# Value loads over all partitions, an accumulated output and halving sums in a fused attention and gated-MLP kernel

## The chip, the cores and the metric

The kernel runs on one core of one Trainium2 chip. The metric is device time in microseconds for one execution; the median of three runs is 217.5 us (216.51 to 218.15). Engine names below: PE is the matrix engine, PEld its weight load, DVE the VectorE, ACT the ScalarE, POOL the GpSimd, SP the SyncE, which here only issues DMAs. A `DMA_TRANSPOSE` is a DMA that transposes 2-byte data on its way.

## What is computed

```python
def _A_ref(x, wqkv, wo):                 # S 2048, D 512, 32 heads of 16
    W, dil = 8, 2                        # key w of row s is row s - 2 w
    q, k, v = split(x @ wqkv)
    logits = einsum("bhsd,bhswd->bhsw", q, kg) * Dh ** -0.5   # masked where s - 2 w < 0
    attn = softmax(logits, axis=-1)
    o = einsum("bhsw,bhswd->bhsd", attn, vg)
    return o @ wo

def _B_ref(x, w1, w2, w3, w4):           # F 1376
    h = gelu(layernorm(x) @ w1)
    hs = concat(h's four column groups, shifted by +1, -1, +2, -2 rows) @ w2
    x1 = x + hs
    return x1 + gelu(layernorm(x1) @ w3) @ w4

x = A_x
xn = layernorm(x)
s = _A_ref(xn, A_wqkv, A_wo)
g = silu(_B_ref(xn, B_w1, B_w2, B_w3, B_w4))
return x + s * g
```

All inputs and the output are bf16; the output is 2048 rows of 512.

## The kernel before

The 2048 rows are cut into 16 tiles of 128 rows (index `i`) and 4 chunks of 512 rows (index `c`, four tiles each). The weights lie in SBUF from the start on. Nothing is scheduled by a planner at build time: the string `ORDER` lists some 810 steps, `name.arguments`, and the loop at line 700 issues them one after the other. Each engine, and each engine's DMA queue, works through its own instructions in that order and stops at the first whose inputs are not ready or whose buffer is not free. So a step that waits holds up all that stands behind it on its engine, SP's queue included, which carries nearly all loads and every transpose.

The steps, in the order in which a tile goes through them:

- `ldx`, `ldxc` load x (tiles 0 to 3 one by one, then whole chunks); `ldqk`, `ldv`, `ldw1` to `ldw4`, `ldwo` load weights. `st` takes the row statistics of x on DVE, `rs` and `r2` turn them into 1/std on POOL, `nm` normalizes on ACT into `xr[i]`, `xT` transposes that by DMA into `xnT`. Chunk 0 goes a shorter way over PE (`nm0`, `tr0`, `ev0`).
- `qk` (8 blocks a chunk) and `v` are PE products; `eqk` and `ev` copy them out of PSUM on ACT. `sv` writes the value tile to `v_dram` in DRAM, by a POOL DMA, in (dim, head) order.
- `pw(c, u)` multiplies q by k shifted by 2u rows on DVE (128x2048 elements); `lg(c, u)` sums over head dims with 16 small PE products into the PSUM tile `lg` (8 offsets x 128 rows, heads and tiles on partitions). `smx` subtracts the maximum (DVE), `ex` exponentiates (ACT), `sms` sums over the offsets and inverts (DVE), `smn` multiplies, reordering into `E_n`, and `tE` transposes `E_n` by two DMAs into `att`.
- `vl(i, u)` loads the value rows of tile `i` shifted by 2u from `v_dram`: partition group u % 4 (32 partitions), in four blocks of 32 rows. Eight loads of 128 KB fill the buffer `vs` of one tile; there are three such buffers. `vp` multiplies `vs` by `att` on DVE, `ws` sums over the offsets with 8 PE products against the 0/1 matrix `sel`, `eo` copies out, `oTr` transposes two tiles by DMA, `wo` is the last product of the attention. The last two tiles go over PE instead (`oTp`, `eoT`).
- `w1`, `eh`, `hTr`, `w2`: the first part of the MLP, with the shifts as column offsets of `hT`; `xa` adds the residual on DVE, `st3s`, `r3`, `nm3`, `x1Tr` are its second normalization and transpose; `w3` (11 blocks a chunk), `eg`, `w4` (11 products a tile), `ya`, `si` give g in `xr[i]`.
- `sg` multiplies s (PSUM) by g on DVE into `xr[i]`; `fag` on POOL or `fav` on DVE adds x; `so` writes the 128 rows of the tile to the output.

PSUM has six banks `mm0` to `mm5` for products and the `lg` tile; the last argument of a PE step is its bank. A bank is free again once DVE or ACT has read it, which is how a late DVE instruction stops PE.

The lines that the change touches are 475 to 522 (softmax), 616 to 644 (value loads, product, sum), 145 to 171 and 187 (the buffers of x), 277 (`sel`), 693 (`fag`) and `ORDER`.

Of the kernel before, what the change touches and what calls it, by code (L numbers as in the profile page):

```python
# [8 lines left out]
AF = mybir.ActivationFunctionType  # L9
ALU = mybir.AluOpType  # L10
# [30 lines left out]
w2.8.3 ev.11 st3s.10 hTr.12 w3.0.9.0 smx.1 sv.11 vl.5.1 v.14.2 eg.0.9 vl.5.2 vl.3.7 w3.0.1.4
vl.4.3 xa.8 w3.0.6.0 vl.4.0 eg.0.1 st3s.6 vl.4.2 w2.12.3 vl.3.0 eg.0.6 st3s.5 r3.3 vl.4.7 ev.14
w3.0.5.4 pw.2.2 vl.5.3 ex.1 vl.3.1 w2.13.2 vl.5.6 xa.12 vl.5.5 w3.0.8.0 st3s.8 vl.3.3 vl.5.4
xa.13 sv.14 w3.0.4.3 nm3.6 vl.3.5 r3.2 st3s.12 vl.5.0 eg.0.8 w3.0.3.2 st3s.13 vl.3.2 vl.4.4
w3.0.0.1 sms.1 vl.5.7 w3.0.2.5 eg.0.3 vl.4.1 eg.0.5 xT.15 w3.0.7.2 r3.6 eg.0.2 vp.3 w3.0.10.4
eg.0.7 eg.0.4 lg.2.1 lg.2.2 eg.0.10 lg.2.0 w2.11.3 eg.0.0 pw.2.3 nm3.5 w4.0.1 nm3.4 xa.11 nm3.7
x1Tr.2 smn.1 st3s.11 pw.2.5 w4.3.3 r3.5 tE.1.0 ya.0 tE.1.1 pw.2.4 si.0 qk.3.7.1 x1Tr.3 ya.3
w4.2.4 eqk.3.7 si.3 vp.5 qk.3.3.1 v.15.3 eqk.3.3 ya.2 w3.1.0.2 vp.4 ev.15 w1.15.4 nm3.10 sv.15
eg.1.0 qk.3.0.3 qk.3.1.1 eh.15 qk.3.6.5 nm3.11 hTr.15 ws.5.4 eqk.3.0 ws.4.2 eo.5 vl.8.5 ws.3.3
vl.7.4 lg.2.5 eo.3 qk.3.4.4 vl.6.6 eo.4 vl.6.0 si.2 qk.3.5.3 vl.7.6 vl.6.1 w2.15.2 vl.7.0 vl.6.4  # L50
eqk.3.5 w2.14.0 xa.15 vl.6.7 eqk.3.6 vl.6.3 w4.1.3 eqk.3.1 st3s.15 vl.8.4 eqk.3.4 xa.14 vl.6.5
vl.7.3 st3s.14 vl.8.6 vl.7.5 w3.1.10.0 r3.7 ya.1 vl.7.7 vl.6.2 w3.1.7.4 eg.1.10 vl.8.0 vl.7.2
w3.1.1.3 vl.8.3 vl.8.2 w3.1.3.1 eg.1.7 vp.6 vl.8.7 w3.1.6.0 vl.8.1 eg.1.3 oTr.1 w3.1.4.4 eg.1.6
w3.1.5.1 eg.1.4 vl.7.1 ws.6.0 x1Tr.5 eg.1.5 lg.2.3 eg.1.1 lg.2.4 pw.2.6 w3.1.8.1 si.1 vl.9.4
wo.0.3 pw.2.7 vl.9.2 vl.9.7 wo.1.4 eo.6 vl.9.0 vp.7 eg.1.8 vl.9.3 wo.3.0 oTr.2 wo.2.5 nm3.15
qk.3.2.1 sg.3 vl.9.6 nm3.14 sg.2 fag.3 vl.9.1 ws.7.0 eqk.3.2 sg.1 vl.9.5 lg.2.6 eo.7 lg.2.7
vl.10.6 w3.1.9.1 pw.3.0 fag.2 vl.10.1 vl.10.3 w3.1.2.0 fag.1 eg.1.9 smx.2 vl.10.2 vl.10.4 w2.9.4
eg.1.2 vl.10.5 so.g.2 vl.10.7 w4.4.0 so.g.1 oTr.3 so.g.3 sg.0 ex.2 xa.9 fag.0 pw.3.2 x1Tr.7
w4.7.4 so.g.0 st3s.9 vl.10.0 ya.4 r3.4 sms.2 si.4 lg.3.0 w4.6.0 pw.3.3 nm3.9 smn.2 w4.5.3 nm3.8
pw.3.1 tE.2.1 ya.6 x1Tr.4 ya.7 lg.3.3 si.6 lg.3.1 wo.4.0 ya.5 si.7 pw.3.6 tE.2.0 si.5 wo.5.3  # L60
sg.4 wo.6.4 sg.5 fag.4 wo.7.0 sg.6 nm3.13 w3.2.2.3 pw.3.4 fag.5 nm3.12 w3.2.9.4 x1Tr.6 eg.2.2
so.g.4 vp.10 w3.2.5.1 fag.6 w3.2.4.5 eg.2.5 so.g.5 so.g.6 w3.2.3.3 sg.7 eg.2.4 vp.8 fag.7
ws.10.0 eg.2.3 lg.3.2 eg.2.9 vl.13.2 w3.2.1.5 so.g.7 eo.10 vl.13.1 vl.13.7 w3.3.0.4 eg.2.1 vp.9
vl.13.6 vl.13.5 w3.2.8.0 eg.3.0 vl.13.0 w3.2.7.5 vl.13.4 eg.2.8 vl.13.3 pw.3.5 w3.2.6.4 eg.2.7
lg.3.6 eg.2.6 lg.3.4 lg.3.5 pw.3.7 w3.2.10.5 w3.2.0.4 eg.2.10 lg.3.7 eg.2.0 ws.9.5 smx.3 ws.8.0
eo.9 vl.12.5 w4.10.4 vl.11.3 eo.8 vl.11.7 oTr.4 ex.3 w4.8.0 ya.10 vl.11.4 vl.11.1 vl.11.0 si.10
vl.11.5 sms.3 vl.11.2 w4.11.4 vl.11.6 vl.12.4 vl.12.2 ya.8 vl.12.7 smn.3 si.8 vl.12.1 wo.8.0
ya.11 tE.3.1 vp.11 w4.9.5 si.11 vl.12.0 vl.12.6 vl.12.3 tE.3.0 sg.8 w3.3.5.4 ya.9 fag.8 w3.3.8.0
si.9 eg.3.5 wo.9.5 so.g.8 w3.3.4.3 sg.9 vp.12 w3.3.2.1 fag.9 eg.3.4 w3.3.10.4 eg.3.2 so.g.9
eg.3.8 w3.3.6.3 eg.3.10 vp.13 ws.12.0 eg.3.6 w3.3.9.4 eo.12 vl.15.1 vl.15.0 w3.3.1.0 vl.15.3  # L70
eg.3.9 vl.15.2 w3.3.7.3 vl.15.4 eg.3.1 vl.15.5 w3.3.3.4 eg.3.7 vl.15.7 vl.15.6 ws.11.0 eg.3.3
ws.13.3 eo.11 vl.14.6 w4.15.4 vl.14.5 eo.13 vl.14.0 vp.15 vl.14.7 oTr.5 w4.14.3 ya.15 oTr.6
# [8 lines left out]
def kernel(  # L81
# [32 lines left out]
    U4 = 4  # L114
    T32 = 32
    NB = P // T32
    NPW, NVS, NH3, NVT, NHT = 3, 3, 12, 3, 3

    x2 = A_x.flatten_outer_dims()
    out2 = out.flatten_outer_dims()  # L120
# [613 lines left out]
```

## Time and profile before

| | |
|---|---|
| median of the runs | 217.5 us (216.51 to 218.15) |
| the profiled execution | 216.87 us, of which the span is 215.1 |
| PE, DVE, ACT, POOL busy | 190.6, 161.6, 132.2, 78.8 us |
| granted PE clock | 0.99 of full speed |
| DMA: SP's queue, share of 16 engines' span | 33.24 MB, 70.8% |
| DMA: POOL's queue | 3.95 MB, 6.0% |
| value loads `vs<-v_dram` | 128 of 128 KB, 3.6 us median from issue to landing (2.1 to 7.5) |
| value stores `v_dram<-vt` | 16 of 128 KB, 3.7 us median |
| output stores from POOL | 14 of 128 KB, 2.7 us median |
| `DMA_TRANSPOSE` `xnT<-xr` | 12, 3.9 us median (2.4 to 8.4) |

The page is of one execution. Matmuls are pipelined, so that their busy times overlap; the pace of PE is read from the distance of starts. A group line gives the source line, the engine, the operation, what is written and read, how often, then busy us and mean ns of one, then the idle time just before and what ended it.

### The profile page before, as it was taken

The numbers are of one execution on the slowest core, as the hardware profiler recorded it, in microseconds if no ns is written. First come the engines' busy times: TensorE is split into PE (matmuls) and PEld (weight loads), VectorE is DVE, ScalarE is ACT, GpSimd is POOL, SyncE is SP. The second block draws the span as 40 slices with busy tenths as digits, with TensorE's granted clock in tenths as the row PEclk, the third lists the DMA queues.
The fourth block names the chain that finished last, engine by engine and source line by source line (L and its number), as shares of the span: only waits on it lengthen the run. The fifth ranks groups of instructions, "written<-read, shape, count | busy, mean of one in ns | idle before, by whom it ended". The sixth has DMA issues, their size and how long they took to land.

```text
span 215.1 us, 3828 instructions
## 1 busy us (share of the span) xinstructions
PE 190.6 (89%) x1408; PEld 85.5 (40%) x1408; DVE 161.6 (75%) x203; ACT 132.2 (61%) x198; POOL 78.8 (37%) x129
## 2 busy tenths in 40 slices
PE   6899769999897989996999979988988996998990
PEld 1444323444342434452444434434444442443440
DVE  4887977199798399969933369999999686826593
ACT  3267865687848825992499588743764950972240
POOL 7146974621163402712310202940691001700282
PEclk9999988999999999999999999999999999999999
DMA  6999998899847698993317999992536499079212
GB/s 197 362 290 378 342 166 197 220 203 247 136 98 123 142 202 193 251 167 73 73 33 213 239 226 214 215 235 47 96 119 184 110 213 167 24 224 221 70 49 98
DMA packets 63011, 37.95 MB, mean 176 GB/s; under 512 B 38371, under 2 KB 61521, under 8 KB 62993
## 3 DMA queue, kind: packets, MB, share of 16 engines
q1 hardware_dynamic: 60976, 33.24, 70.8%
q0 software_dynamic: 1472, 3.95, 6.0%
q10 hardware_dynamic: 544, 0.52, 0.8%
q8 instruction: 11, 0.18, 0.3%
q14 instruction: 8, 0.06, 0.1%
HBM read 24.84 MB, written 4.21 MB: 135 GB/s over the span
## 4 chain that ended last, share of the span: by engine, by line
DVE 29%; PE 28%; DMA 19%; SPq 11%; issue 6%; POOL 3%; ACT 2%; DVEq 0%; ACTq 0%; POOLq 0%
SPq L620 9%; DVE vs L629 8%; DMA vs<-v_dram 7%; DVE pw L456 6%; PE mm L376 6%; PE mm L582 5%; PE mm L400 4%; DMA xnT<-xr 4%; DMA xc<-in_A_x_dram 3%; PE mm L599 3%; PE mm L641 3%; PE mm L679 2%; DVE xr L686 2%; DVE st L299 2%; DVE ssum L497 2%
## 5 line engine op out<-in xcount | busy, mean ns | idle before, releaser
L629 DVE TENSOR_TENSOR vs<-vs,att 128x4096 bf16<-128x4096 bf16 x16 | 39.6, 2487 | 15.1 <-DMA vs<-v_dram 13.7
L456 DVE TENSOR_TENSOR pw<-qT,kT 128x2048 bf16<-128x2048 bf16 x32 | 39.1, 1258 | 12.4 <-ACT kT L385 5.9
L582 PE MATMUL mm<-x1T,w_sb 128*128 128x512 bf16 (+1 forms) x176 | 40.7, 379 | 1.8 <-DVE xr L686 1.7
L599 PE MATMUL mm<-w_sb,h 128*128 128x512 bf16 (+1 forms) x176 | 39.9, 379 | 2.5 <-DVE xr L538 1.7
L591 ACT ACTIVATE h<-mm 128x512 bf16<-128x512 f32 (+1 forms) x44 | 25.2, 597 | 13.5 <-PE mm L582 13.2
L694 POOL TENSOR_TENSOR xr<-xc,xr 128x512 bf16<-128x512 bf16 x9 | 17.6, 1958 | 42.3 <-DVE xr L686 42.2
L376 PE MATMUL mm<-xnT,wqk_sb 128*128 128x512 bf16 x128 | 30.4, 384 | 0.6 <-DVE xr L606 0.6
L599 PEld LDWEIGHTS <-h 128*128 128x128 bf16 (+1 forms) x176 | 16.9, 98 | 23.8 <-issue 3.9
L582 PEld LDWEIGHTS <-w_sb 128*128 128x128 bf16 (+1 forms) x176 | 17.2, 100 | 22.2 <-issue 2.8
L610 ACT ACTIVATE xr<-xr 128x512 bf16<-128x512 bf16 x16 | 10.0, 632 | 23.9 <-DVE xr L606 23.7
L418 POOL DMA_DIRECT2D v_dram<-vt x16 | 9.7, 605 | 36.9 <-ACT vt L410 36.7
L400 PE MATMUL mm<-wv_sb,xnT 128*128 128x512 bf16 x64 | 18.4, 414 | 2.2 <-DMA xnT<-xr 1.5
L376 PEld LDWEIGHTS <-wqk_sb 128*128 128x128 bf16 x128 | 12.4, 99 | 16.2 <-issue 2.0
L531 PE MATMUL mm<-w_sb,hT 128*128 128x512 bf16 x64 | 16.1, 379 | 1.3 <-DMA hT<-ht 1.1
L425 PE MATMUL mm<-w_sb,xnT 128*128 128x512 bf16 x64 | 15.8, 379 | 1.2 <-ACT ht L435 1.2
L329 POOL TENSOR_SCALAR ve<-mv 128x2 f32<-128x2 f32 (+1 forms) x11 | 4.2, 379 | 34.3 <-DVE mv L543 28.0
L538 DVE TENSOR_TENSOR xr<-mm,xr 128x512 bf16<-128x512 f32 x16 | 10.7, 677 | 7.4 <-PE mm L531 7.4
L559 ACT ACTIVATE xn<-xr,nmr,rstd 128x512 bf16<-128x512 bf16 x16 | 12.4, 813 | 5.4 <-POOL nmr L336 4.0
L679 PE MATMUL mm<-wo_sb,oT 128*128 128x512 bf16 x64 | 15.3, 379 | 0.3 <-DVE xr L606 0.3
L467 PE MATMUL lg<-pw,e_log 128*32 128x128 bf16 x512 | 12.5, 223 | 3.3 <-DVE pw L456 3.2
L330 POOL TENSOR_TENSOR rstd<-ve,mhalf 128x2 f32<-128x2 f32 (+1 forms) x15 | 14.7, 980 | 1.2
L410 ACT ACTIVATE vt<-mm 128x512 bf16<-128x512 f32 x16 | 9.5, 594 | 7.2 <-PE mm L400 6.9
(71 smaller groups left out, 247.0 us busy)
## 6 DMA issues: line engine op xcount, KB each, us to landing
vs<-v_dram SPq DMA_DIRECT2D x128, 128.0 KB, 3.6
v_dram<-vt POOLq DMA_DIRECT2D x16, 128.0 KB, 3.7
out_dram<-xr POOLq DMA_DIRECT2D x14, 128.0 KB, 2.7
xc<-in_A_x_dram SPq DMA_DIRECT2D x3, 512.0 KB, 9.0
w_sb<-in_B_w_dram SPq DMA_DIRECT2D x2, 688.0 KB, 10.6
w_sb<-in_B_w_dram SPq DMA_DIRECT2D x2, 640.0 KB, 10.6
wqk_sb<-in_A_wqkv_dram SPq DMA_DIRECT2D x2, 512.0 KB, 6.0
wv_sb<-in_A_wqkv_dram ACTq DMA_DIRECT2D x2, 256.0 KB, 3.7
```

Source lines behind the costliest of these rows:

```text
L376: nc.tensor.matmul(pt, lhsT=wqk_sb[:, dt, nt * P : (nt + 1) * P], rhs=xnT[c][:, :, dt, :], start=(dt == 0), stop=(dt == ND - 1),)
L400: nc.tensor.matmul(pt, lhsT=xnT[c][:, jj, dt, :], rhs=wv_sb[:, dt, :], start=(dt == 0), stop=(dt == ND - 1),)
L425: nc.tensor.matmul(pt, lhsT=xnT[c][:, jj, dt, :], rhs=w1_sb[:, dt, :], start=(dt == 0), stop=(dt == ND - 1),)
L456: nc.vector.tensor_tensor(out=pw_t[c, u], in0=q_t[c], in1=k_t[c][:, :, DIL * u : DIL * u + CH], op=ALU.mult)
L531: nc.tensor.matmul(pt, lhsT=hT[:, g, r0 : r0 + P], rhs=w2_sb[:, g, :], start=(g == 0), stop=(g == ND - 1),)
L582: nc.tensor.matmul(pt[:fs, :], lhsT=w3_sb[:, dt, ft * P : ft * P + fs], rhs=x1T[c][:, :, dt, :], start=(dt == 0), stop=(dt == ND - 1),)
L591: nc.scalar.activation(h3[c, ft][:fs, :], mm.pop(("w3", c, ft))[:fs, :], AF.Gelu_apprx_tanh)
L599: nc.tensor.matmul(pt, lhsT=h3[c, ft][:fs, jj * P : (jj + 1) * P], rhs=w4_sb[:fs, ft, :], start=(ft == 0), stop=(ft == NF - 1),)
L620: nc.sync.dma_start(out=vs[i][T32 * (u % U4) : T32 * (u % U4) + T32, :, u // U4, :], in_=v_dram[r0 : r0 + P, :].rearrange("(b t) d -> t b ...
L629: nc.vector.tensor_tensor(out=vv, in0=vv, in1=att[c][:, :, H * jj : H * jj + H].unsqueeze(2).to_broadcast([P, NB * 2, DH, H]), op=ALU.mult,)
L679: nc.tensor.matmul(pt, lhsT=oT[i // 2][:, i % 2, dt, :], rhs=wo_sb[:, dt, :], start=(dt == 0), stop=(dt == ND - 1),)
L694: nc.gpsimd.tensor_tensor(out=xr[i], in0=xtile(i), in1=xr[i], op=ALU.add)
```

## The change

- `vl` becomes `vl(i, h, b)`: one load covers offsets 4h to 4h+3 of the 32 rows of block b, on all 128 partitions (partition 4t + u for row t, offset u). The source is an access pattern whose rows overlap. There are again eight loads of 128 KB a tile. `E_n`, `sel`, `vp` and `ws` follow that layout.
- Thirteen tiles of the output are first filled with x by four DRAM-to-DRAM copies (`pre`); `soa` then adds `s * g` to them by an accumulating DMA from POOL, in place of `fag` and `so`. Tiles 13, 14 and 15 still go by `fav` and `so`.
- `sms` adds halves (512, 256, 128 elements a partition) in place of one strided reduction; `smn` becomes two instructions.
- Chunks 1 and 3 of x share a buffer; there are 14 buffers for `h3` in place of 12.
- `ORDER` is made anew. Some of what moves: `ldw3` and `ldw1` change places among the first loads, `ldqk.s.0` comes after `ldqk.s.1`, `ldw3.s.0`, x's chunk 1 and `ldw4.s.2`; `st.4` and `st.5` come ahead of `st.8`; `ldxc.s.3` and `ldw4.s.1` come later; the softmax of chunk 0 comes after more of the products.

```diff
-NPW, NVS, NH3, NVT, NHT = 3, 3, 12, 3, 3
+NPW, NVS, NH3, NVT, NHT = 3, 3, 14, 3, 3
...
-    x_t = [fixed(f"x{i}", [P, D]) for i in range(TPC)] + [
-        fixed(f"xc{c}", [P, TPC, D]) for c in range(1, NCH)
-    ]
+    x_t = [fixed(f"x{i}", [P, D]) for i in range(TPC)]
+    x_c = {}
...
     def ldxc(q, c):
+        x_c[c] = rot("xc", c, 2, [P, TPC, D])
...
     def c_sel():
-        nc.gpsimd.tensor_tensor(out=sel_f, in0=ident[:, 0:64], in1=ident[:, 64:128], op=ALU.add)
-        nc.gpsimd.tensor_tensor(out=sel, in0=sel_f[:, 0:32], in1=sel_f[:, 32:64], op=ALU.add)
+        idu = ident.rearrange("p (t u) -> p t u", u=U4)
+        nc.gpsimd.tensor_tensor(out=sel_f, in0=idu[:, :, 0:2], in1=idu[:, :, 2:4], op=ALU.add)
+        nc.gpsimd.tensor_tensor(out=sel, in0=sel_f[:, :, 0], in1=sel_f[:, :, 1], op=ALU.add)
...
     def sms(c):
+        lg_t.pop(c)
+        s4 = rot("s4", 0, 1, [P, 4, P], F32)
+        nc.vector.tensor_tensor(
+            out=s4, in0=E_c[c][:, 0:4, :], in1=E_c[c][:, 4:8, :], op=ALU.add
+        )
+        nc.vector.tensor_tensor(out=s4[:, 0:2, :], in0=s4[:, 0:2, :], in1=s4[:, 2:4, :], op=ALU.add)
         ssum = rot("ssum", 0, 1, [P, P], F32)
-        nc.vector.tensor_reduce(
-            out=ssum, in_=E_c[c].rearrange("p u t -> p t u"), axis=AX.X, op=ALU.add
-        )
+        nc.vector.tensor_tensor(out=ssum, in0=s4[:, 0, :], in1=s4[:, 1, :], op=ALU.add)
...
     def smn(c):
-        E_n[c] = rot("E_n", c, 2, [P, NB, W, T32])
-        nc.vector.tensor_tensor(
-            out=E_n[c],
-            in0=E_c.pop(c).rearrange("p u (b t) -> p b u t", t=T32),
-            in1=sm.pop(c).rearrange("p (b t) -> p b t", t=T32).unsqueeze(2).to_broadcast([P, NB, W, T32]),
-            op=ALU.mult,
-        )
+        E_n[c] = rot("E_n", c, 2, [P, 2, NB, T32, U4])
+        e_in = E_c.pop(c)
+        r_in = sm.pop(c).rearrange("p (b t) -> p b t", t=T32)
+        for h in range(2):
+            nc.vector.tensor_tensor(
+                out=E_n[c][:, h],
+                in0=e_in[:, U4 * h : U4 * h + U4, :].rearrange("p u (b t) -> p b t u", t=T32),
+                in1=r_in.unsqueeze(3).to_broadcast([P, NB, T32, U4]),
+                op=ALU.mult,
+            )
...
     def tE(c, h):
-            in_=E_n[c][:, 2 * h : 2 * h + 2, :, :].rearrange("p b u t -> p (b u t)"),
+            in_=E_n[c][:, h].rearrange("p b t u -> p (b t u)"),
...
-    def vl(i, u):
+    def vl(i, h, b):
         if i not in vs:
-            vs[i] = rot("vs", i, NVS, [P, NB, 2, D])
-        r0 = i * P + DIL * u
-        nc.sync.dma_start(
-            out=vs[i][T32 * (u % U4) : T32 * (u % U4) + T32, :, u // U4, :],
-            in_=v_dram[r0 : r0 + P, :].rearrange("(b t) d -> t b d", t=T32),
-        )
+            vs[i] = rot("vs", i, NVS, [P, 2, NB, D])
+        src = bass.AP(
+            tensor=v_dram.tensor,
+            offset=v_dram.offset + (i * P + T32 * b + DIL * U4 * h) * D,
+            ap=[[D, T32], [DIL * D, U4], [1, D]],
+        )
+        nc.sync.dma_start(out=vs[i][:, h, b, :], in_=src)
...
-    def fag(i):
-        nc.gpsimd.tensor_tensor(out=xr[i], in0=xtile(i), in1=xr[i], op=ALU.add)
+    def pre(q, i, n):
+        qs[q].dma_start(
+            out=out2[i * P : (i + n) * P, :].rearrange("(p r) d -> p (r d)", p=P),
+            in_=x2[i * P : (i + n) * P, :].rearrange("(p r) d -> p (r d)", p=P),
+        )
+
+    @step
+    def soa(i):
+        nc.gpsimd.dma_start(out=out2[i * P : (i + 1) * P, :], in_=xr[i], accum_op=ALU.add)
```

The list around the softmax of the last chunk and to the end, as it becomes:

```diff
+lg.3.7 vl.11.0.0 ws.9.2 eo.8 sg.4 lg.3.5 eo.9 vl.12.1.2 ws.10.5 lg.3.6 soa.4 eo.10 vl.13.0.2
+wo.7.3 smx.3 vl.13.1.2 eg.2.9 vl.13.0.1 wo.6.5 vl.13.0.0 vl.12.1.0 w4.9.4 vl.13.1.3 sg.7 ex.3
+vl.12.0.1 sg.6 vl.13.1.1 soa.7 vl.13.1.0 soa.6 vl.12.0.2 w4.11.5 ya.9 vl.12.1.3 vl.12.0.3 sms.3
+si.9 vl.11.1.1 vl.11.1.3 vl.11.1.2 w4.8.4 vl.11.0.3 ya.11 vl.11.0.2 smn.3 si.11 w4.10.5 ya.8
+tE.3.1 si.8 vl.11.1.0 vl.11.0.1 w3.3.9.4 oTr.4 ya.10 w3.3.8.3 si.10 vl.13.0.3 eg.3.9 w3.3.6.5
+vl.12.0.0 vp.11 vl.12.1.1 w3.3.4.2 tE.3.0 eg.3.6 w3.3.1.0 eg.3.8 wo.8.5 eg.3.1 eg.3.4 ws.11.3
+sg.8 wo.9.2 eo.11 vl.14.0.3 vp.12 soa.8 vl.14.0.1 w3.3.7.3 vl.14.0.2 vl.14.1.0 w3.3.5.5 eg.3.7
+vl.14.1.2 sg.9 oTr.5 w3.3.10.0 eg.3.5 vp.13 soa.9 w3.3.3.2 eg.3.10 vl.14.0.0 vl.14.1.3 w3.3.2.5
+eg.3.3 vl.14.1.1 ws.12.0 eg.3.2 ws.13.2 eo.12 vl.15.1.0 w4.14.5 vl.15.1.1 eo.13 oTr.6 vl.15.0.2
+vp.14 wo.11.2 vl.15.0.3 vl.15.1.2 w4.13.0 vl.15.0.0 vl.15.0.1 vl.15.1.3 sg.11 ya.14 soa.11
+ws.14.2 ya.13 si.14 w4.15.5 vp.15 si.13 eo.14 wo.13.0 ya.15 w4.12.2 sg.13 si.15 fav.13 so.s.13
+ws.15.0 ya.12 wo.10.5 si.12 eo.15 oTp.14.2 sg.10 wo.12.3 eoT.14 soa.10 oTp.15.5 sg.12 wo.14.2
+eoT.15 soa.12 wo.15.5 sg.14 fav.14 sg.15 so.s.14 fav.15 so.s.15
```

## The prediction

> **What bounds the kernel now.** First the page's busy shares and some rows of its 40 slices (5.4 us each).
>
> ```profile
> PE 190.6 (89%) x1408; PEld 85.5 (40%) x1408; DVE 161.6 (75%) x203; ACT 132.2 (61%) x198; POOL 78.8 (37%) x129
> ...
> PE   6899769999897989996999979988988996998990
> ...
> DMA  6999998899847698993317999992536499079212
> GB/s 197 362 290 378 342 166 197 220 203 247 136 98 123 142 202 193 251 167 73 73 33 213 239 226 214 215 235 47 96 119 184 110 213 167 24 224 221 70 49 98
> ```
>
> PE is the fullest engine. I count its least work from the chain of waits, where four 512-column products take 0.86 us: 736 of them are 158.6 us, 32 logit steps (0.37) 11.8, 16 window reductions (0.49, half of "L641 x16 0.98") 7.8, the transposes 2.2; 180.4 of the 215.1 us span. The first transpose starts at 5.7 and the last product ends at 208.9, so 22.8 us between them are stalls. Read from the timeline, start to start less 0.216 us, those above 0.4 are: 4.2 us at 23 to 30; 3.9 at 47, 58, 65 and 77 (mostly behind DMA transposes); 2.6 at 97 and 101; 1.6 at 125; 3.6 at 142, 148, 157 and 164; 1.9 at 180; 1.1 at 197.
>
> Next, who waits, from the table of waits (total, times, longest), and one stretch of the chain in order of time (start, length):
>
> ```profile
> DVE vs L629 <- DMA vs<-v_dram: 13.7, 4, 5.2
> ```
> ```profile
> 89.33 0.43 SPq L620
> 89.81 5.49 DMA vs<-v_dram
> 95.38 2.29 DVE vs L629
> ...
> 98.81 0.60 DVE xr L538
> ...
> 121.02 3.71 DMA vs<-v_dram
> ...
> 175.70 3.08 DMA vs<-v_dram
> ...
> 191.77 3.21 DMA vs<-v_dram
> ```
>
> Before each of the four waits SP issues a burst of value loads 0.475 us apart, and the last lands 3.1 to 5.5 us later. VectorE stands still, then multiplies (L629), and only then frees the PSUM bank that PE waits for. The windows over such a burst (busy time of PE, PEld, DVE, ACT, POOL; clock; DMA share; GB/s) say why:
>
> ```profile
> 88.00:90.00 2.00, 1.88 (x10) 0.78 (x9) 1.93 (x6) 1.98 (x3) 1.65 (x5) 1.00 1.17 231
> 117.00:119.00 2.00, 2.00 (x11) 0.88 (x9) 1.90 (x5) 1.98 (x5) 0.00 (x0) 1.00 1.00 244
> ```
>
> The DMA engines are full at 231 to 244 GB/s: 128 KB takes 0.57 us, longer than the 0.475 between issues. In the second slice, when x and weights with the same 1 KB rows arrive on 128 partitions, they move 362 GB/s, 0.36 us per 128 KB.
>
> Last, the groups of instructions (busy, mean ns | idle before):
>
> ```profile
> L629 DVE TENSOR_TENSOR vs<-vs,att 128x4096 bf16<-128x4096 bf16 x16 | 39.6, 2487 | 15.1 <-DMA vs<-v_dram 13.7 <-DMA att<-E_n 1.4
> L694 POOL TENSOR_TENSOR xr<-xc,xr 128x512 bf16<-128x512 bf16 x9 | 17.6, 1958 | 42.3 <-DVE xr L686 42.2
> L497 DVE TENSOR_REDUCE ssum<-E_c 128x128 f32<-128x1024 bf16 x4 | 7.6, 1912 | 0.5 <-ACT E_c L492 0.5
> L507 DVE TENSOR_TENSOR E_n<-E_c,rinv 128x1024 bf16<-128x1024 bf16 x4 | 2.7, 681 | 0.0
> L690 DVE TENSOR_TENSOR xr<-xc,xr 128x512 bf16<-128x512 bf16 x3 | 2.7, 896 | 0.1
> ```
>
> L629 takes 2.29 us undisturbed, but 3.24, 2.63, 3.24 and 3.25 where GpSimd's final add (L694) runs beside it; a pw product beside it took 2.56 instead of 1.2, two L690 adds 1.11 and 1.15 instead of 0.42. Together 6.1 us of VectorE's time.
>
> **Part by part.** The sum is made against the profiled execution, 216.87 us (span 215.1 and 1.8 around it); the median of the three runs is 217.5, 0.6 above it.
>
> *Value loads.* Still 128 issues of 128 KB, so SP's 0.475 each stays. Per burst of 16 the queue no longer grows by 16 x (0.57 - 0.475) = 1.5 us, and the last load should land as the quickest x load did, in 2.3 us. The four waits shorten by 3.2, 1.4, 0.8 and 0.9. PE's stalls behind them (2.6, 1.6, 1.9, 1.1) give up the smaller of each pair: 2.6 + 1.4 + 0.8 + 0.9 = **-5.7**. Bounds: -7.2, all four; and, if the packets run no faster, 0. I take -5.7, since the 362 GB/s row has the same row size and 128 partitions. What is late next is the issue itself: eight loads need 3.8 us.
>
> The Trainium skill (SBUF — State Buffer, section Door 1: The DMA port swizzle) has partitions 0 to 31 reach 8 of 16 SBUF ports, 189 against 328 GB/s at 1 MiB. By those figures 128 KB goes from 0.69 to 0.40 us, an estimate that would make this term larger; the trace's 0.57, with loads for all four groups in flight, disagrees with 0.69.
>
> *Output by accumulating DMA.* Thirteen GpSimd adds go, so VectorE's 6.1 us of sharing goes. At 139 to 164 it held PE up: the stalls at 142 and 148 are 1.5 us against 1.4 us of slowing just before, 0.9 at 157 against 1.0, 1.2 at 164 against 1.3, together **-3.5** (bounds -3.6 and, if the new order leaves VectorE no hurry there, 0). Thirteen accumulating DMAs replace the thirteen plain output DMAs from GpSimd (0.56 us to issue, 1.7 to 5.2 to land); what they add to the landing is hidden except for the last. rstd steps queue behind them on GpSimd, which loses 23 us of adds, so I put that at 0.
>
> *Tail.* Now 6.2 us from the last product to the end. With an undisturbed L690: 0.68 + 0.42 + 3.3 (end of the last add to end of span) = 4.4. But soa.12's product ends about 1.2 us before the last one; issue 0.57 to 1.1, landing 2.3 to 5.2 and 1.2 to close make 2.9 to 6.3 after the last product. I take 4.8: **-1.4** (-1.8 to +0.1).
>
> *Prefill of the output.* Four DRAM-to-DRAM copies, 1.7 MB, at 231 to 362 GB/s 5 to 7 us of all rings. Three stand in SP's queue ahead of hTr.15 and x1Tr.3, which w2.14 and w3.1 wait for; PE has 3.5 and 5.3 us of other work there, against 1.25 to issue, 2.6 to 3.3 to land and about 2 of copy. I take **+1.0** (0 to +5).
>
> *Softmax sums.* The reduction (1.91) becomes adds of 512, 256 and 128 elements. A 512-element op at one element per cycle took 0.68 (L538), 1024 took 1.23 (L485): 0.68 + 0.41 + 0.27 = 1.36, so -0.55 per chunk. The E_n product becomes two of 512 elements with the inner step 128 on one operand and 0 on the other. From L507 each would be 0.34, from L538 0.68, from the reduction that reads the same tile at the same step (1.91 for 1024) 0.95. I take 0.68, the nearest in size and kind: +0.68 per chunk. Net +0.13 per chunk, **+0.5** (-2.2 to +2.7).
>
> The Trainium skill (VectorE: DVE Perf Modes, section What auto-detection actually checks) speaks against this edit: two elements per cycle only where every tensor is 16-bit with step 1. The old L507 row, 681 ns for 1024, ran at two per cycle; by the rule the new pair loses that, about 1.4 us, and without it 0.7.
>
> *Start of the list.* st.4 and st.5 move ahead of st.8, so chunk 1's rstd comes three statistics (3 x 0.79 = 2.4 us) earlier, and xT.5 stands behind 6.6 MB of loads instead of 7.8. In the chain that transpose took 8.39 us (start 21.19). Of the 4.2 us of stalls there 2.5 follow the pw products' own pace (1.2 each on VectorE) and stay; 1.7 wait for this transpose: **-1.7** (-4.2 to +1, since qk.0's weights now come behind 3.5 MB instead of 1.8).
>
> *The rest of the order.* Its cover is counted in products. After lg.3.6 PE has 22 us until ws.12 (2 wo, 4 w4, 10 w3, wo.8, ws.11, wo.9), against about 14 for smx, ex, sms, smn, tE and vp. vl.14 and vl.15 need 3.8 + 1.25 + 2.3 + 2.3 = 9.7 and have 12. But from vp.5 to smx.3 the list has 47.5 us of VectorE work against 45.7 of PE, so VectorE becomes the bound there: **+1.8** (0 to +6, each wait inside it counting in full). The 3.9 us behind transposes I leave.
>
> Sum: -5.7 - 3.5 - 1.4 + 1.0 + 0.5 - 1.7 + 1.8 = -9.0, to **207.9 us**.
>
> **Rivals.**
> 1. *VectorE is the bound from vp.5 to the end.* If the strided product costs 0.95 a half (+2.2 over the four chunks) and what is saved by sharing turns into idle time elsewhere (-3.5 lost), 207.9 + 5.7 = 213.6. For it: VectorE at 9.9 to 10 of 10 us at 130 to 160 now. Against: 6.1 us of sharing go there.
> 2. *The loads' gain is hidden.* If the issue pace alone sets when values come, the -5.7 goes, and the new list's tighter middle costs its upper +6 in place of 1.8 only in part (+2): 215.6. For it: SP issues are 11% of the chain; against: DMA is 19%.
> 3. *Slower: the value rows collide.* The new load reads only 38 distinct rows, each up to four times, with all 16 engines at once; the old one read 128. If such reads queue up in DRAM, 128 KB takes longer. At 0.57 us the gain is nil; above it each 0.1 us adds 1.6 per burst in four waited bursts, 6.4 us. Without the load term the rest is -3.3, so it turns slower from 0.57 + 0.05 us; at 0.70 it is 213.6 + 8.3 = 221.9. No row shows such reads; for it stands nothing but that, against it that every read is still a whole 1 KB row.
>
> **Numbers.** Forecast 0.60 (its own range 203 to 212), rival 1 0.13, rival 2 0.10, rival 3 0.17. About 1% (2.2 us) is what a measurement here can tell from no change. Faster by more: 0.73; within: 0.10; slower: 0.17. The low end is the forecast with the start's, the softmax's and the loads' better bounds taken in part, 202.5; the high end takes in rivals 1 and 2, 217.5; left out is rival 3 and a little below.
>
> **What would show it.** Value loads landing in about 2.3 us with DMA share under 1 in the bursts; DVE's wait for vs under 7 us instead of 13.7; L629's mean at 2.29; E_n halves at 0.68; the first xT landing in about 5 us; four copies of about 2 us each; under 5 us after the last product. It is wrong if value packets take as long as before, if transposes behind the copies land after 5 us or more, or if VectorE's idle time moves behind att and w4 instead of going.

## The result, and the profile after

The changed kernel takes 226.8 us (median of 4 runs, 226.01 to 229.61) beside 217.35 for the kernel before (216.51 to 218.15): a ratio of 1.042, 95% interval 1.036 to 1.049. It is slower by 9.5 us, where 9.6 less was forecast. The profiled execution took 229.61 us, 2.8 above the median, with a span of 227.8. Executions of one kernel scatter by some per cent, and one of the kernel tE_accum_sums below took 326.25 us at a clock of 0.573, so medians and ranges here are of all executions and ratios of the quicker ones alone.

From the page of the changed kernel, the busy share of PE and its slices (5.7 us each), the granted clock, and what the DMA engines did:

```profile
PE 197.3 (87%) x1408; PEld 86.3 (38%) x1408; DVE 160.1 (70%) x215; ACT 130.0 (57%) x198; POOL 64.2 (28%) x115
...
PE   6798999699669859999999499589989999699982
...
PEclk9999999999979979999999889979999999889999
DMA  6999986648778548699957238974780596699505
GB/s 222 354 341 299 250 197 169 172 107 171 214 156 129 106 114 207 184 207 210 272 146 184 46 79 212 205 210 109 186 138 3 140 235 182 160 186 219 127 23 92
```

PE is still the fullest engine, but its row now has a 4 and two 5s, and the clock, 0.99 over the span before, is 0.96, with slices of 7 and 8 after the holes. VectorE and GpSimd do less than before, and still the span is longer. What PE and the others wait for, from the table of waits (total, times, longest):

```profile
DVE vs L642 <- DMA vs<-v_dram: 14.0, 5, 4.3
ACT ht L438 <- DMA hT<-ht: 7.2, 4, 4.1
PE mm L594 <- DMA x1T<-xn: 4.7, 2, 3.6
DVE vs L642 <- DMA att<-E_n: 4.3, 2, 3.3
PE mm L543 <- DMA hT<-ht: 3.9, 1, 3.9
```

VectorE's wait for values did not shrink (13.7 before). What grew are the waits for DMA transposes: for `att`, `hT` and `x1T`, the longest now 3.3 to 4.1 us. Before, no such wait of PE, VectorE or ScalarE was longer than 2.5:

```profile
ACT ht L435 <- DMA hT<-ht: 3.6, 3, 2.5
DVE vs L629 <- DMA att<-E_n: 1.4, 1, 1.4
```

Their place in SP's queue says why. SP's timeline (start, length, line, how many in a row):

```profile
117.44 3.83 SPq L636 DMA_DIRECT2D vs<-v_dram  x6
121.37 1.22 SPq L530 DMA_TRANSPOSE att<-E_n  x1
...
133.18 10.51 SPq L636 DMA_DIRECT2D vs<-v_dram  x15
143.79 1.40 SPq L581 DMA_TRANSPOSE x1T<-xn  x1
```

The chain that ended last goes through just these transposes (start, length):

```profile
60.84 3.94 DMA hT<-ht
...
121.37 2.58 DMA att<-E_n
124.07 2.29 DVE vs L642
128.41 2.57 PE mm L692 x8
...
143.79 5.15 DMA x1T<-xn
148.99 4.39 PE mm L594 x12
...
168.68 7.07 PE mm L594 x32
```

Six loads hold SP until 121.27; the transpose of `E_n` that vp.5 needs is issued only then, vp.5 starts at 124.07, and PE, which had started a product at 124.7, starts the next at 128.41, 3.45 us late. Fifteen loads hold SP for 10.5 us in front of x1Tr.5; PE loses 3.76 us at 145.0. At 60.8 the same happens to hTr.4 behind six loads and one of the output copies: 4.06 us. The last two lines show a second price. After the stall at 145 twelve products take 4.39 us, 0.37 each; the 32 at 168.68 take 0.22 each. The windows over the stretches behind two such stalls (busy time of PE, PEld, DVE, ACT, POOL; granted clock; DMA share; GB/s) show the clock at 0.83:

```profile
60.00:70.00 10.00, 6.10 (x25) 2.10 (x26) 5.72 (x9) 2.47 (x4) 0.00 (x0) 0.83 0.63 139
150.00:160.00 10.00, 10.00 (x90) 4.36 (x88) 6.24 (x7) 6.99 (x9) 1.60 (x2) 0.83 0.58 150
```

Ten microseconds at a mean clock of 0.83 are about 1.7 us of work lost, on top of the stall. Windows of 2 us show five stretches of 3.4 us at half clock while products run, from 64.6, 81.7, 129.5, 150.0 and 197.7, behind stalls of 4.06, 3.17, 3.45, 3.76 and 1.9 us; the kernel before has one, from 30.5. The Trainium skill (TensorE: Matmul & The Clock Gate, section Part 1: The HAM clock gate) says that the clock falls to half after an idle window of about 3.4 us and comes back after as long a busy one. The trace agrees on the length of the slow stretch, and on that of the stall in four cases of five. Counted by starts of products, PE's stalls above 0.9 us add up to 13.8 us before and 23.5 after, 9.7 of the 12.7 us by which the span of the profiled execution grew.

The source of it is one number. One line of the source at a time, the issue of a value load on SP (ns, minimum, median, maximum) and its landing, first before and then after:

```profile
L620 SPq DMA_DIRECT2D vs<-v_dram x128: 302/430/1225, 22.8 to 198.3; - x128
...
DMA to landing us min/median/max: 2.1/3.6/7.5
```
```profile
L636 SPq DMA_DIRECT2D vs<-v_dram x128: 513/602/1819, 27.7 to 211.5; - x128
...
DMA to landing us min/median/max: 2.2/2.9/6.0
```

The load lands sooner, 2.9 us against 3.6, but SP needs 0.60 us instead of 0.43 to issue it, 0.65 from one to the next instead of 0.475. All 128 issues together took 82.4 us of SP's queue against 59.1.

The groups that the prediction costed (busy, mean ns | idle before):

```profile
L642 DVE TENSOR_TENSOR vs<-vs,att 128x4096 bf16<-128x4096 bf16 x16 | 36.4, 2288 | 18.3 <-DMA vs<-v_dram 14.0 <-DMA att<-E_n 4.3
L714 POOL DMA_DIRECT2D out_dram<-xr x13 | 11.6, 951 | 56.9 <-DVE xr L699 56.6 <-issue 0.2
L519 DVE TENSOR_TENSOR E_n<-E_c,rinv 128x512 bf16<-128x512 bf16 x8 | 7.9, 1032 | 0.0
L503 DVE TENSOR_TENSOR s<-E_c 128x512 f32<-128x512 bf16 x4 | 2.8, 690 | 6.3 <-ACT E_c L495 6.2
L506 DVE TENSOR_TENSOR s<-s 128x256 f32<-128x256 f32 x4 | 1.7, 425 | 0.1
L508 DVE TENSOR_TENSOR ssum<-s 128x128 f32<-128x128 f32 x4 | 1.2, 292 | 0.1
```

The product of the values runs undisturbed, 2.29. The halving adds take 0.69 + 0.43 + 0.29 = 1.41 us a chunk; one half of the `E_n` product takes 1.03, and an accumulating DMA 0.95 of GpSimd's queue.

### The profile page after: what moved, and what is told of

Its sections match the earlier page's. It is cut to its first block, busy times and chain, and to the rows that moved or that the text cites. A ratio compares the mean times of both kernels' runs of the same rounds, so it can differ in the third digit from the quotient of the medians.

```text
span 227.8 us, 3805 instructions
## 1 busy us (share of the span) xinstructions
PE 197.3 (87%) x1408; PEld 86.3 (38%) x1408; DVE 160.1 (70%) x215; ACT 130.0 (57%) x198; POOL 64.2 (28%) x115
## 4 chain that ended last, share of the span: by engine, by line
PE 38%; DMA 13%; DVE 13%; POOL 9%; SPq 9%; ACT 9%; issue 6%; DVEq 0%; POOLq 0%; ACTq 0%
PE mm L594 9%; PE mm L611 6%; SPq L636 6%; PE mm L692 4%; DMA hT<-ht 4%; DMA x1T<-xn 4%; PE mm L379 4%; PE mm L403 4%; POOL rstd L333 3%; PE mm L654 3%; PE mm L543 3%; DMA vs<-v_dram 3%; PE mm L428 3%; POOL nmr L339 2%; DVE vs L642 2%
## 5 line engine op out<-in xcount | busy, mean ns | idle before, releaser
L642 DVE TENSOR_TENSOR vs<-vs,att 128x4096 bf16<-128x4096 bf16 x16 | 36.4, 2288 | 18.3 <-DMA vs<-v_dram 14.0
L594 PE MATMUL mm<-x1T,w_sb 128*128 128x512 bf16 (+1 forms) x176 | 43.2, 394 | 4.7 <-DMA x1T<-xn 4.7
L459 DVE TENSOR_TENSOR pw<-qT,kT 128x2048 bf16<-128x2048 bf16 x32 | 37.7, 1215 | 9.5 <-ACT kT L388 5.3
L603 ACT ACTIVATE h<-mm 128x512 bf16<-128x512 f32 (+1 forms) x44 | 24.6, 596 | 17.3 <-PE mm L594 17.2
L379 PE MATMUL mm<-xnT,wqk_sb 128*128 128x512 bf16 x128 | 30.9, 387 | 3.2 <-ACT o L667 3.0
L714 POOL DMA_DIRECT2D out_dram<-xr x13 | 11.6, 951 | 56.9 <-DVE xr L699 56.6
L692 PE MATMUL mm<-wo_sb,oT 128*128 128x512 bf16 x64 | 17.5, 408 | 5.0 <-DVE xr L618 3.3
L543 PE MATMUL mm<-w_sb,hT 128*128 128x512 bf16 x64 | 17.5, 410 | 4.0 <-DMA hT<-ht 3.9
L438 ACT ACTIVATE ht<-mm,rstd 128x512 bf16<-128x512 f32 x16 | 10.7, 685 | 12.7 <-DMA hT<-ht 7.2
L333 POOL TENSOR_TENSOR rstd<-ve,mhalf 128x2 f32<-128x2 f32 (+1 forms) x15 | 15.6, 1038 | 1.2
```

Source lines behind the costliest of these rows:

```text
L333: nc.gpsimd.tensor_tensor(out=dst, in0=ve[:, 0:n], in1=mhalf[:, 0:n], op=ALU.pow)
L379: nc.tensor.matmul(pt, lhsT=wqk_sb[:, dt, nt * P : (nt + 1) * P], rhs=xnT[c][:, :, dt, :], start=(dt == 0), stop=(dt == ND - 1),)
L459: nc.vector.tensor_tensor(out=pw_t[c, u], in0=q_t[c], in1=k_t[c][:, :, DIL * u : DIL * u + CH], op=ALU.mult)
L543: nc.tensor.matmul(pt, lhsT=hT[:, g, r0 : r0 + P], rhs=w2_sb[:, g, :], start=(g == 0), stop=(g == ND - 1),)
L594: nc.tensor.matmul(pt[:fs, :], lhsT=w3_sb[:, dt, ft * P : ft * P + fs], rhs=x1T[c][:, :, dt, :], start=(dt == 0), stop=(dt == ND - 1),)
L603: nc.scalar.activation(h3[c, ft][:fs, :], mm.pop(("w3", c, ft))[:fs, :], AF.Gelu_apprx_tanh)
```

## The experiments

The theory after this reading (Q): the new load costs SP 0.17 us more to issue, and in the one queue that also carries every transpose this delays the transposes behind the loads. The rivals: the new list is the harm (L); the strided `E_n` product and the copies are the harm (E); the values' landing is (the forecast's own rival 3). Kernels with old loads also have the old layout of `E_n`, `sel`, `vp` and `ws`; where both fixed x buffers and more `h3` buffers were wanted, the small tile `warm` shares a buffer of `E_c`. Times are medians in us; the kernel before measured 217.0 to 217.8 beside them.

| run | what it is | time (range) | ratio to before (95%) |
|---|---|---|---|
| oldlist_newops | the change in the old order | 225.88 (223.91 to 225.99) | 1.039 (1.032 to 1.046) |
| newlist_oldops | new order only | 214.62 (211.87 to 215.38) | 0.985 (0.976 to 0.994) |
| oldlist_loads | new loads only | 228.88 (226.61 to 230.28) | 1.049 (1.039 to 1.058) |
| newlist_oldloads | all but the new loads | 216.35 (212.05 to 216.53) | not given |
| plainsrc | the change, loads from 128 consecutive rows | 208.92 (207.07 to 213.23) | 0.952 (0.942 to 0.962) |
| oldloads_slowEn | newlist_oldloads, strided product, strided write | 219.45 (217.59 to 221.98) | 1.008 (1.003 to 1.012) |
| transposes_first | the change, three transposes moved | 218.06 (216.22 to 220.91) | 1.006 (1.001 to 1.011) |
| oldops_tE | newlist_oldops, one transpose moved | 209.56 (207.65 to 210.17) | 0.962 (0.954 to 0.970) |
| gapsrc | plainsrc's rows, named in three dimensions | 225.96 (one) | |
| tE_accum_sums | newlist_oldloads, one transpose moved | 210.1 (208.69 to 326.25) | 0.964 (0.956 to 0.972) |
| tE_accum | the same, old sums | 210.23 (208.01 to 213.32) | 0.963 (0.951 to 0.974) |
| expanded | oldops_tE, values stored four times, 32 loads | 224.35 (221.45 to 226.71) | 1.023 (1.012 to 1.035) |
| plainsrc_tf | plainsrc and transposes_first together | 214.1 (211.01 to 216.83) | 0.982 (0.965 to 0.998) |
| expanded_late | expanded, loads later, transposes ahead | 224.03 (223.93 to 229.11) | 1.041 (1.029 to 1.052) |

**Which part is the harm.** Four kernels cross the two lists with the old and the new operations. The edits are the halves of the change: `ORDER` alone, the new operations alone in the old `ORDER` (the output copies stand behind x1Tr.3 there), and `vl` with its layout alone. One step of each kind is shown.

```diff
 # newlist_oldops: the new list, each step in its old form
-vl.5.1.2  soa.3  pre.s.0.4
+vl.5.6  fag.3 so.g.3
 # oldlist_loads: the old list, only the loads in their new form
-vl.5.6
+vl.5.1.2
```

> The old list of steps with all the new operations (each value load of the old list replaced by one of the new form, the four prefill copies put behind the fourth x1T transpose, where SP has nothing else). Theory Q (the new value loads take SP 0.65 us each instead of 0.475, and in SP's one queue they delay the transposes behind them): 218 to 224 us, SP's loads again 0.65 apart. Theory L (the new list is the harm, the operations are good): 208 to 216 us. Theory E (the strided E_n product and the copies are the harm): 220 to 226 us with VectorE late before att.

> The new list with all the old operations: old value loads, GpSimd final adds and plain output DMAs, the reduction, one E_n product, no prefill. Theory Q: the loads are back at 0.475 and the transposes come in time, 212 to 219 us. Theory L: the list alone keeps 223 to 228 us. Theory E: 212 to 219 us, as Q.

> The old list, and of the operations only the new value loads with the layout that follows from them (sel, E_n product in two halves, E_n transposes). Theory Q: 218 to 223 us. Theory L: 210 to 216 us, since packets take 46 ns instead of 74. Theory E: 219 to 223 us, 4 x 1.4 us more on VectorE, some of it hidden.

> The changed kernel with nothing but the value loads and their layout put back to the old form; new list, prefill, accumulating output and halving adds stay. Theory Q: 212 to 219 us, the wait of PE for x1T at 145 us gone. Theory L: 223 to 228 us. Theory E with the copies as its main part: 221 to 226 us; with the E_n product as its main part: 213 to 219 us.

The new list without the new operations is not slower but a little faster, 214.62, so L falls. The new loads alone, in the old list, cost more than the whole change: 228.88. With all but the loads the kernel is about as fast as before (three executions of 216.2 to 216.5 and one of 212.05). The harm is in the loads and their layout. Two times lie above Q's ranges: 225.88, which fits E's, and 228.88, which fits none. In the old list the harm takes two ways. VectorE's wait for values grows from 13.7 to 17.7 us, where eight loads need 5.2 us instead of 3.8. Of PE's two largest stalls one, 3.0 us, goes back to values 5.8 us late, the other, 3.6 us, to a transpose of `E_n`.

**Issue or landing.** If the harm is how SP issues the load and not what it moves, a load of the same 128 KB to the same 128 partitions with a plainer source must be free of it. It reads 128 consecutive rows, so the values are not the reference's.

```diff
-        src = bass.AP(
-            tensor=v_dram.tensor,
-            offset=v_dram.offset + (i * P + T32 * b + DIL * U4 * h) * D,
-            ap=[[D, T32], [DIL * D, U4], [1, D]],
-        )
+        r0 = i * P + DIL * U4 * h
+        src = v_dram[r0 : r0 + P, :]
```

> The changed kernel with one difference: the value load of 128 KB reads 128 consecutive rows in place of the overlapping pattern (32 rows by 4 offsets), so its values are not those that the reference asks for; size, destination, number and place in the list stay. Theory Q with the source pattern as the cause of the slow issue: SP's loads are back at 0.43 us each (0.475 apart) and the time falls to 212 to 219 us. If the 128-partition destination is what makes the issue slow: 0.60 stays and the time stays at 223 to 229. Theory E (the E_n product): no change, 223 to 229 us, whatever the issue costs.

208.92, against 226.8 with the overlapping source, and lower than Q's 212 to 219. The same line of the source in this kernel, VectorE's wait for values (that for `E_n`'s transpose is 0.2 us instead of 4.3), and SP's timeline over the stretch that held x1Tr.5 (the profiled execution took 213.23 us):

```profile
L633 SPq DMA_DIRECT2D vs<-v_dram x128: 319/430/2156, 27.1 to 194.8; - x128
...
DMA to landing us min/median/max: 2.0/3.3/5.1
```
```profile
DVE vs L639 <- DMA vs<-v_dram: 7.9, 3, 3.7
```
```profile
125.86 6.96 SPq L633 DMA_DIRECT2D vs<-v_dram  x13
132.92 1.23 SPq L581 DMA_TRANSPOSE x1T<-xn  x1
```

The issue is back at 0.43, thirteen loads take 7.0 us where fifteen took 10.5, and the transpose is issued at 132.92 instead of 143.79. The landing is slower than with the slow issue (3.3 against 2.9), so the landing does not explain the gain. But this kernel differs in two ways, in the shape of the pattern and in the rows (128 different ones instead of 38, each up to four times). The next one reads the same 128 rows as plainsrc, once each, but names them in three dimensions:

```diff
-            offset=v_dram.offset + (i * P + T32 * b + DIL * U4 * h) * D,
-            ap=[[D, T32], [DIL * D, U4], [1, D]],
+            offset=v_dram.offset + (i * P + DIL * U4 * h) * D,
+            ap=[[D, T32], [T32 * D, U4], [1, D]],
```

> The changed kernel with each value load reading 128 consecutive rows of 1 KB, once each, but named in three dimensions (32 rows, then 4 steps of 32 rows, then the row) for a 128-partition destination; the values are therefore not the reference's. Issue on SP was 0.602 us median with rows 8 apart that repeat between the steps, and 0.430 with 128 rows in two dimensions. If the shape of the source (three dimensions against a destination of 128 partitions) makes the issue slow: 0.60 median again, and 218 to 230 us. If it is the repeated or scattered rows: 0.43 median and 207 to 213 us, as with two dimensions.

```profile
L636 SPq DMA_DIRECT2D vs<-v_dram x128: 513/602/1403, 27.6 to 208.2; - x128
...
DMA to landing us min/median/max: 2.3/2.9/5.3
```

0.602 median again, to the nanosecond, and 225.96 us (one execution). Not the overlap of the rows and not the memory, but the form of the pattern sets the issue time, and with it the kernel's. Three dimensions as such are not slow: the old load had three on both sides (32 partitions, 4 blocks, a row; 0.430), and a load of 512 KB in the run "expanded", 128 partitions by 4 blocks on both sides, took 0.50. In the two slow kernels the source walks 32 x 4 rows while the destination walks 128 partitions. And the source of gapsrc is, step for step, that of the old load: 32 rows, by four steps of 32 rows. So neither this source alone (0.430 in the old load) nor 128 partitions alone (0.430 in plainsrc) makes the issue slow, but the two together. Why that costs more is not shown.

**What was in the way on SP.** If the delay of transposes is how the issue time becomes kernel time, moving them ahead of the loads must give much of it back with the issue still at 0.60. Moved were the three behind which PE lost most: hTr.4 to behind eh.4, tE.1.1 to behind tE.1.0, x1Tr.5 to behind nm3.11.

```diff
-nm3.11 ws.4.4 vp.6 w4.0.3 si.2 vl.7.1.3 eo.5 vl.7.0.3
+nm3.11 x1Tr.5 ws.4.4 vp.6 w4.0.3 si.2 vl.7.1.3 eo.5 vl.7.0.3
...
-pw.2.6 tE.1.0 w2.8.1 xa.13
+pw.2.6 tE.1.0 tE.1.1 w2.8.1 xa.13
```

> The changed kernel with three DMA transposes moved up in the list, ahead of the value loads that they stood behind: hTr.4 right after eh.4, tE.1.1 right after tE.1.0, x1Tr.5 right after nm3.11. All operations and the 0.65 us per load stay. Theory Q (the loads harm through SP's queue, by what stands behind them): the stalls of 4.1, 3.5 and 3.8 us at 61, 125 and 145 us go or shrink, 214 to 221 us. If the value loads' own lateness is the harm: 223 to 229 us, since the loads come still later.

218.06: 8.7 us back from three steps of the list, half of the 17.9 that the quick issue brings. PE's wait for `x1T` falls from 4.7 to 0.9 us, its 3.9 us for `hT` go, and VectorE's wait for `att` falls from 4.3 to 2.8. VectorE's wait for values stays (13.9 us), with loads as slow to issue as before. Put together with the plain source:

> The changed kernel with the three transposes ahead of the loads (218.06) and with 128 consecutive rows in two dimensions as source of each load (values not the reference's). Issue 0.43 instead of 0.602, 128 x 0.17 = 22 us of SP's queue less. If the issue time still harms through other transposes and late loads: 205 to 209 us, 9 or more below 218.06. If the three transposes were all of it: 214 to 218. The loads' gain of the forecast exists if it is below 210.1 (old loads, tE.1.1 moved, the other edits in) by 2 or more after the strided product's 3 us; if it is 209 to 212, the quicker landing is worth no more than the strided product costs.

214.1, but with a wide scatter, 211.0 to 216.8: at the lower end of what was expected if the three transposes were all of it (214 to 218), 4 us under transposes_first and 5 above plainsrc. The two remedies do not add up. What is shown is that the three transposes carry 8.7 of the 17.9 us. The rest is not taken apart; VectorE's wait for values is part of what differs, 13.9 us with the slow issue and 7.9 and 8.0 in the two kernels with the quick one. In plainsrc_tf PE stands 4.2 us at 75.8 behind an eviction by ACT (3.2 at 75.6 in plainsrc), and ACT stands there behind GpSimd's row statistics; that is 1 us of the 5 by which the pair is slower, the others stay open.

**The strided product.** Into newlist_oldloads goes the new product's reading order, at two instructions a chunk:

```diff
-        nc.vector.tensor_tensor(out=E_n[c], in0=..., in1=..., op=ALU.mult)
+        for h in range(2):
+            nc.vector.tensor_tensor(
+                out=E_n[c][:, :, U4 * h : U4 * h + U4, :].rearrange("p b u t -> p b t u"),
+                in0=e_in[:, U4 * h : U4 * h + U4, :].rearrange("p u (b t) -> p b t u", t=T32),
+                in1=r_in.unsqueeze(3).to_broadcast([P, NB, T32, U4]),
+                op=ALU.mult,
+            )
```

> The changed kernel with the old value loads and their layout, as before, but the E_n product still made in two halves that read with step 128 and a broadcast of step 0, so each half should take about 1.03 us. Against the same without the halves (216.35 us): theory E 219 to 224 us; theory Q 216 to 219 us.

219.45 beside 216.35: 3 us above the median of newlist_oldloads, 7 above its quickest execution. That lies in E's range, 219 to 224. But the edit did more than was meant. In the old layout the product writes with a step too, and a half took 2.52 us instead of 1.03:

```profile
L514 DVE TENSOR_TENSOR E_n<-E_c,rinv 128x512 bf16<-128x512 bf16 x8 | 18.6, 2515 | 0.0
```

VectorE has 15.9 us more to do than with the old product (2.7), where the change has 5.2 more (7.9). So this run does not give the price of the change's product; with three times its extra work it cost 3 to 7 us. What clears the product of being the cause is the pair above: plainsrc and gapsrc both have it at 1.03 us and lie 17 us apart.

**Output and sums.** In newlist_oldops and newlist_oldloads the largest stall was the same one, behind tE.1.1 (3.5 us at 116.1). With that one step moved, the list serves as a ground on which the two other edits can be measured.

> The new list with all old operations (214.62 us), and tE.1.1 moved right behind tE.1.0, ahead of six value loads. Its largest stall, 3.5 us at 116 us, is vp.5 waiting for that transpose with ya.1 behind it. Theory Q: that stall goes, 210 to 213 us. Otherwise 213 to 216 us.

> New list with tE.1.1 behind tE.1.0, old value loads and layout; output by prefill and accumulating DMA and softmax sums by halving adds, as in the change. Against the same kernel with the old output and old sums (209.56). The recorded forecast has these two edits at -3.5 -1.4 +1.0 -2.0: 203 to 205 us. If they are worth nothing, since neither is on the path to the end: 208 to 211. If accumulating does harm (slow issue on GpSimd's queue, prefill in front of transposes): 212 to 218, as in the run with tE.1.1 at its place in the new list (216.35).

> As the kernel with halving adds of this batch, but with the old reduction for the softmax sums. The halving adds took 1.41 us a chunk against 1.91, so four chunks give 2.0 us on VectorE. If VectorE is what the path waits for in those stages: 1 to 2 us longer than with halving adds; if not: within 1 us of it. Against 209.56 (same list, old output) the difference is what accumulating is worth.

209.56 with the old output and sums; 210.23 with the accumulated output; 210.1 with the halving adds as well. One step moved in the list is worth 5 us, and there neither of the two edits is worth anything that can be told apart. Moving that step helped on both grounds: all three are faster than both kernels of the case, at a ratio of 0.96. In the profile of the first the clock row is 9 in every slice but the last, and between the ninth slice and the last PE's row stays at 8 or 9:

```profile
PE   6699799969999998899999999999999999999980
...
PEclk9999999999999999999999999999999999999998
```

**Fewer issues.** If SP's queue is the scarce thing, fewer and larger loads should pay. The ground is oldops_tE (209.56), with the layout and the strided product of the change. Here the value tile is stored four times in DRAM, in the order of the loads, by one DMA with a repeated source (`dst` names the four places), so that one load of 512 KB fills 128 partitions in four blocks: 32 loads instead of 128, their issues 19.9 us of SP in all instead of 59 or 82.

```diff
-        nc.gpsimd.dma_start(out=v_dram[PADK + i * P : PADK + (i + 1) * P, :], in_=vt.pop(i))
+        nc.gpsimd.dma_start(out=dst, in_=vt.pop(i).unsqueeze(1).to_broadcast([P, U4, D]))
...
-        nc.sync.dma_start(out=vs[i][:, h, b, :], in_=src)
+        r0 = (i * P + DIL * U4 * h) * U4
+        nc.sync.dma_start(
+            out=vs[i][:, h, :, :],
+            in_=v_dram[r0 : r0 + NB * P, :].rearrange("(b p) d -> p b d", p=P),
+        )
```

> New list with tE.1.1 behind tE.1.0, old output and old sums. Values are stored to DRAM four times, in the order in which the loads want them, by one DMA of 512 KB per tile with a repeated source, so that one value load of 512 KB fills 128 partitions x 4 blocks: 32 loads on SP instead of 128. Theory of SP's queue: 96 issues of 0.43 to 0.60 us are gone from it, so stalls of TensorE on transposes shrink; the strided product costs 3 us (as measured), the copies bring 6.3 MB more writes: 203 to 210 us. If the four-fold store is late for the loads behind it, or its traffic collides with them: 212 to 222.

> As the run with fourfold stores (224.35), but each of the 32 loads stands at the third of the four places that it had in the new list instead of the first, and the three transposes stand ahead. There TensorE lost 6.7 us at 36.6 and 3.1 at 89.5 behind loads that waited on SP for their store. If the places were the harm: those stalls go, 208 to 216 us. If the fourfold stores and 512 KB landings (5.7 us) are the harm: 220 or more, with VectorE waiting longer for values.

224.35 and 224.03: a miss, and not for the reason that the second expectation gave. VectorE hardly waits for values here (0.5 us in the first, 5.3 in the second); PE's stall of 6.7 us at 36.6 in the first is the largest, on SP's timeline and then on that of all engines:

```profile
29.20 2.60 SPq L627 DMA_DIRECT2D vs<-v_dram  x3
31.89 7.41 SPq L445 DMA_TRANSPOSE hT<-ht  x3
```
```profile
42.81 0.69 ACT L439 ACTIVATE ht<-mm,rstd 128x512 bf16<-128x512 f32 x1 [7.76 <-DMA hT<-ht]
...
43.55 2.72 PE L374 MATMUL mm<-xnT,wqk_sb 128*128 128x512 bf16 x6 [6.55 <-ACT ht L439]
```

SP is not at a load that waits for its store: three loads of 512 KB are out by 31.8, and of the three transposes behind them the last took 4.67 us to issue, against 1.2 elsewhere; ACT waits for the buffer that it reads, and PE for ACT. The windows there (columns as above) show DMA engines that are full:

```profile
36.00:40.00 4.00, 1.00 (x5) 0.37 (x4) 0.81 (x3) 0.00 (x0) 2.56 (x8) 1.00 1.07 398
```

So a transpose can be late behind few large loads as behind many small ones: here not SP's time but the full DMA engines, with 512 KB loads and fourfold stores on them, seem to hold it. With loads later and transposes ahead that stall goes, but two `hT` transposes behind four loads take 5.4 us to issue at 52.3 and four `xnT` transposes 7.0 at 58.4, and PE stands 5.6 us at 58.7. How much of this is the loads and how much the 6.3 MB more of stores was not settled.

## Why the prediction was wrong

**The step that failed** is in *Value loads*: "Still 128 issues of 128 KB, so SP's 0.475 each stays." It carried the price of an issue over from a load of another form. The issues cost 0.65, and 128 x 0.175 = 22 us went into a queue that carries the transposes too. What the prediction then named as late next, "the issue itself: eight loads need 3.8 us", was the bound: eight need 5.2. With the issue at 0.43 and everything else as in the change the kernel takes 208.92, with 0.602 and rows read once each 225.96. The path that the sum left out is the one from the issue to the transposes behind it: moving three of them gives back 8.7 us. That 208.92 lies 1.0 from the forecast is in part luck, since the terms of the output, the product and the list came out otherwise, as told below.

**No rival had it.** Rival 3 was the one on the slower side, with rows that collide in DRAM; gapsrc, where no row repeats, is as slow. Rival 2 had the pace of the issues as the limit, but at the old pace, and only as a gain that is hidden. None looked at what stands behind the loads in SP's queue. The 3.9 us of stalls that the prediction did put down mostly to transposes were left, and the clock after a stall was not in the sum at all.

**Landing and packets.** As forecast the packets were quicker: in 134 to 143, inside the burst of fifteen, 46 ns median a 1 KB packet against 82, 54 and 85 in three bursts before and 46 in the fourth (from 88, 117, 171 and 187), and the DMA share fell under 1:

```profile
134.00:143.00 9.00, 9.00 (x43) 4.17 (x42) 6.72 (x9) 6.36 (x8) 3.24 (x6) 1.00 0.80 198
```

But 198 GB/s is only what an issue every 0.65 us brings. In plainsrc, where loads come faster, the rings are full again at 235 GB/s, as before:

```profile
127.00:133.00 6.00, 6.00 (x29) 2.74 (x27) 6.00 (x8) 4.79 (x7) 1.87 (x2) 1.00 1.01 235
```

So the 362 GB/s on which the term rested, read from a slice with x and weights, did not come with the 128 partitions. VectorE's wait for values did fall there, to 7.9 us from 13.7, where the term had 6.3 less. But with the old loads the new list has 7.4 (newlist_oldops) to 12.0 (newlist_oldloads), so the fall need not come from the load. Whether the load as such is worth it is not shown: plainsrc stands at 208.92, the old loads with tE.1.1 moved at 210.1, and plainsrc_tf at 214.1.

**Output.** VectorE's sharing with GpSimd was gone, as forecast (2288 ns, and the output's last adds 0.43 and 0.42). On the ground of the better list it bought nothing (209.56 and 210.23): the lower bound of that term, 0, "if the new order leaves VectorE no hurry there", is what holds there. The accumulating DMA took 0.85 to 1.2 us to issue, inside the bound of 0.57 to 1.1 but for its end, and 3.8 us to land. From the end of the last product to the end of the span it is about 4.5 us, near the 4.8; but counted in the same way the kernel before has 5.4 and not 6.2, so the tail gave 0.9 where 1.4 was forecast.

**Prefill.** The copies landed in 3.3 to 4.8 us and not in about 2. The first, which the term did not count, stands between two groups of loads in front of hTr.4, 0.65 of the 5.6 us between two transposes there. With loads of 0.43 PE still waits there 1.7 us (tE_accum), 2.5 (plainsrc) and 3.0 (newlist_oldloads) for `hT`, against 0.8 at most in the two kernels without the copies (newlist_oldops, oldops_tE); in the whole time this is not seen, 210.23 beside 209.56.

**Softmax.** The adds were right (1.36 forecast, 1.41 measured). A half of the product took 1.03 us where 0.68 was taken and 0.95 was the upper bound. The row that it was nearest to was the reduction over the same tile with the same step, and not the plain product: 4 x 2 x 0.35 = 2.8 us more of VectorE's time than forecast. What of it reaches the kernel's time no run shows. The Trainium skill (VectorE: DVE Perf Modes, section What auto-detection actually checks) gives two elements a cycle only where every tensor is 16-bit with step 1; the trace goes further, since 1.03 us is slower than the 0.69 of the add of 512 elements that writes 32-bit sums.

**Start of the list.** The longest landing of an `xnT` transpose is 5.4 us instead of 8.4, as forecast. The rest of the order was forecast at +1.8; the new list as a whole, with old operations, measured 2.4 us under before.

## What to carry to other kernels

A DMA has a price on the queue that issues it, and here that price went with the form of its access pattern, 0.43 or 0.60 us for the same 128 KB: before replacing a load, find a row in the trace with the new form, and if there is none, bound the issue time as well as the landing. Where one queue carries loads and transposes, multiply the difference by the number of loads and look at which transposes stand behind them; moving a single transpose ahead of six loads was worth 5 us here, where the accumulated output and the halving adds were worth nothing that can be told apart. A stall of 3 to 4 us cost PE more than its own length here, since the clock behind it stood at half for 3.4 us. And an edit that is to copy one cost needs its own row read: the strided product was meant to take 1.03 us a half, and took 2.52.

## What had not been expected

- The issue of a 128 KB load on SP took 0.430 us median with source and destination walked in the same dimensions and 0.602 with a source of 32 x 4 rows for 128 partitions, whether the rows overlapped or not; the 512 KB load with equal dimensions took 0.50.
- VectorE read a bf16 tile with an inner step of 128 elements at 1.03 us for 512 elements, about 2.0 ns each, against 681 ns for 1024 in the old order; with a write of step 32 as well it took 2.52 us.
- The issue of an accumulating DMA on GpSimd took 0.87 us median, against 0.56 for the plain output DMA of the same 128 KB.
